# A fused convolution and mixer kernel: single batches transposed in twos of neighbouring blocks, one group's convolution buffers opened in two steps, first stages in smaller double-buffered pieces

## The chip, the core and the metric

The kernel runs on one core of one Trainium2 chip. Its time is the device time of one execution in microseconds (us); lower is better. The engines are named as in the profile: PE is TensorE's matmul stream and PEld its weight loads, ACT is ScalarE, DVE is VectorE, POOL is GpSimd, SP is SyncE, which here only issues DMAs.

## The reference, cut to what matters

```python
# x (8, 4096, 192), weight (8 heads, 7 taps); w = softmax of weight over the taps
x_pad = concat([zeros(B, 6, D), x], axis=1)
x[b, s, h, g] = sum over k of w[h, k] * x_pad[b, s + k, h, g]     # causal convolution, 24 columns a head
h  = relu(x.T @ w_tok1) @ w_tok2          # token mixing: 4096 -> 256 -> 4096, per batch
u  = x + h.T
h2 = relu(u @ w_ch1) @ w_ch2              # channel mixing: 192 -> 1536 -> 192, per token
out = u + h2
```

All values are float32. The kernel keeps the precision by splitting operands into a rounded part ("hi") and a rest ("lo") and adding three products, hi by hi, hi by lo and lo by hi.

## The kernel before

**Groups.** The eight batches are worked in five groups: batch 0, batch 1, and the pairs 2-3, 4-5 and 6-7. A single batch has `nb == 1`, a pair `nb == 2`. 4096 tokens are 32 blocks of 128; a tile is `TJ` = 4 blocks (512 tokens), and a batch has 8 tiles, q0 to q7.

**First stages** (`stage1`, for one group while the group before it runs its tiles). The convolution runs in four parts of 8 blocks for each batch (q2 = 0 to 3). `load` brings raw tokens, columns in two halves, `raw0` and `raw1`. `taps` gives head by head the first tap to ACT (line 608) and the other six to DVE (line 610), accumulating in `xc`. `store` writes `xc` to DRAM (`xcd`, line 634). Then token mixing's first matmul: for each quad of four blocks, `t1_load` fetches the weights (one `t1` buffer for a pair, two for a single batch), and for the pair 2-3, the first one, `t1_hi` (ACT, line 659) and `t1_lo` (DVE, line 663) split them and a store keeps the split (`t1p`) for later pairs. For pairs `split_hi` (ACT, 675) and `split_lo` (DVE, 679) split `xc` into one buffer `xhl`. `mix` multiplies into two accumulators `ps_a`: line 691 for a single batch, lines 695 to 697 for a pair, 24 matmuls a quad.

**Tiles.** Each tile runs in this order on PE: `channel1` (line 865, 72 matmuls at a time on half-height operands, results through ACT 904 into hi and DVE 905 into lo), `mix2` of the next tile (800 to 805; DVE adds its result to `u`, lines 810 and 812 for a single batch, 815 for a pair), the first half of `channel2` (917 and 918; DVE sums in 921 and 922), `transposed` of the next tile (828 on PE, 830 on ACT for hi, 831 on DVE for lo, into `own`), the second half of `channel2`, and the store. So the transposes of the next tile have the second half of `channel2` between them and the `channel1` that reads them.

A single batch's `u` has every block's 192 columns twice: DVE's second add (812) broadcasts them, so that one 128-row transpose delivers 64 columns in the lower and the same 64 columns in the upper partitions. `channel1` needs them in both places.

**Who sets the order.** `Background` keeps a model clock for PE and one for DVE. Each foreground step calls `fg` with its cost; `fill` then pops items of the next group's first stages from their streams, as long as the model's DVE is not ahead. Items have a `gate` (a time when their input may be there) and a `lag`. What is left when a group's last tile begins is forced by `finish()` ahead of the next group's first `channel1`. Each engine runs its instructions in the order written. The decode of the second token-mixing weights (lines 164 to 180, a staging copy on ACT in 1006, a store in 1008) is also such a stream, in batch 0's tiles.

Of the kernel before, what the change touches and what calls it, by code (L numbers as in the profile page):

```python
# [34 lines left out]
class Background:  # L35
# [28 lines left out]
    def fill(self, until):  # L64
        for s in self.streams:
            while s["items"] and s["items"][0].eager:
                self.pop(s)
        while self.dve < self.pe + until:
# [9 lines left out]
            if not ready:  # L78
                return
# [33 lines left out]
def conv_mixer_kernel(ctx: ExitStack, tc: tile.TileContext, x, weight, w_tok1, w_tok2, w_ch1, w_ch2, out):  # L113
    nc = tc.nc
# [12 lines left out]
    TJ = 4  # L127
    NT = NJ // TJ
# [6 lines left out]
    def f32(ap):  # L135
# [20 lines left out]
        dram.tile([P, len(g), NJ, D], F32, name=f"xcd{i}") for i, g in enumerate(GROUPS)  # L156
# [25 lines left out]
    class Decoder:  # L182
# [27 lines left out]
        def b(self, st, hi, lo, view=lambda v: v):  # L210
            return decode_b(view(st["top"]), hi, lo)

# [142 lines left out]
    def stage1_first(pe, p0, pd, late, load_u, load_next, after, hooks):  # L355
# [21 lines left out]
        xf = xcd[0][:, 0]  # L377
# [119 lines left out]
        def xc_store(c):  # L497
            nc.gpsimd.dma_start(out=xf[:, chunks[c].start:chunks[c].stop], in_=xcs[c])
# [76 lines left out]
    def stage1(gi, pool):  # L575
# [13 lines left out]
        def load(q2, part):  # L589

            ds = slice(part * DH, (part + 1) * DH)
            raw = pool.tile([P, RB + HALO, nb, DH], F32, name=f"raw{part}")
# [31 lines left out]
        def taps(q2, h, k):  # L624
            st = states[q2]
            if k == 0 and h == 0:
                st["xc"] = pool.tile([P, RB * nb, D], F32, name="xc", bufs=2)
# [3 lines left out]
        def store(q2):  # L631
            xc = states[q2]["xc"].rearrange("p (j b) d -> p j b d", b=nb)
            for i in range(nb):
                nc.gpsimd.dma_start(out=xcd[gi][:, i, q2 * RB:(q2 + 1) * RB], in_=xc[:, :, i])
            mark("conv", q2)

        def t1_load(n):
            q2, q = divmod(n, RB // TJ)
            js = slice(q * TJ, (q + 1) * TJ)
# [5 lines left out]
            if nb == 1:  # L645
                t1 = mp.tile([P, TJ, 1, JT], F32, name="t1", bufs=2)
                nc.sync.dma_start(out=t1, in_=part(top))
            elif gi == 2:
                t1 = mp.tile([P, TJ, 2, JT], F32R, name="t1")
                nc.sync.dma_start(out=f32(t1[:, :, 1:2]), in_=part(top))  # L650
            else:
                t1 = mp.tile([P, TJ, 2, JT], F32R, name="t1")
# [8 lines left out]
        def t1_lo(q2, q):  # L661
            t1 = states[q2]["t1", q]
            nc.vector.tensor_tensor(out=t1[:, :, 1], in0=f32(t1[:, :, 1]), in1=f32(t1[:, :, 0]), op=ALU.subtract)
            js = slice(q * TJ, (q + 1) * TJ)
# [4 lines left out]
        def split_hi(q2, q):  # L669
            st = states[q2]  # L670
            v = st["xc"][:, q * TJ * nb:(q + 1) * TJ * nb, :]
            xhl = mp.tile([P, 2, TJ * nb, D], F32R, name="xhl")
# [9 lines left out]
        def mix(q2, q, kc):  # L682
            t1 = states[q2]["t1", q]
            ms = slice(kc * P, (kc + 1) * P)
            for j in range(TJ):
                n = q2 * RB + q * TJ + j
                a, z = n == 0, n == NJ - 1
                ps = accs[kc][:, :nb * D]
                if nb == 1:
                    xc = states[q2]["xc"]  # L690
                    nc.tensor.matmul(out=ps, lhsT=t1[:, j, 0, ms], rhs=xc[:, q * TJ + j, :], start=a, stop=z)  # L691
# [9 lines left out]
        last_q = RB // TJ - 1  # L701
        for part in range(2):
            convolving.append(Item(lambda part=part: begin(0, part), eager=True))
        mixing.append(Item(lambda: t1_load(0), eager=True))
        for q2 in range(NS):
            for h in range(0, H, 2):
                for k in range(K):
                    it = Item(lambda a=(q2, h, k): taps(*a), cost=2 * (RB * nb * G / 0.96 + 130) if k else 0)
                    if h % HH == 0 and k == 0:
                        it.lag = 100  # L710

                        def gate(q2=q2, h=h):
                            if h == 0 and q2 > 1 and ("split" if nb > 1 else "mixed", q2 - 2, last_q) not in done:
                                return None
                            return done["load", q2, h // HH] + 2e3 + 2e3 * nb

                        it.gate = gate
                    convolving.append(it)
# [3 lines left out]
            for q in range(last_q + 1):  # L722
                a = (q2, q)
                n = q2 * (last_q + 1) + q
                if gi == 2:
                    mixing.append(Item(lambda a=a: t1_hi(*a), lag=300, gate=lambda n=n: done["t1", n] + (5e3 if n else 14e3)))
                    mixing.append(Item(lambda a=a: t1_lo(*a), cost=TJ * JT / 0.96, lag=1300))
                if nb > 1:
                    mixing.append(Item(lambda a=a: split_hi(*a), lag=300, gate=lambda q2=q2: done.get(("conv", q2))))
                    mixing.append(Item(lambda a=a: split_lo(*a), cost=TJ * nb * D / 0.96, lag=500 + 700 * nb))  # L730
# [46 lines left out]
    def tokens(u, i):  # L777
        return u[:, :, :, i]
# [338 lines left out]
```

## Time and profile before

| | us |
|---|---|
| median of 3 runs (lowest, highest) | 2102.41 (2100.42, 2102.64) |
| the profiled execution, its own time | 2103.08 |
| its span in the profile | 2101.3 |
| PE busy | 2059.8 (98%) |
| DVE busy | 1344.5 (64%) |
| ACT busy | 731.4 (35%) |

The span runs from the first to the last instruction of the profiled execution; the 1.8 us beside it in that execution's own time lie around the span. PE is busy nearly everywhere; DVE is close to full in the first quarter of the span, where batch 0's tiles share it with the convolution of batch 1 and the weight decode, and less so behind it.

### The profile page before, as it was taken

Reading aid. Unit: us, or ns where it says so; the run is one execution under the profiler, and the core shown is the slowest. Engines: PE = TensorE matmul, PEld = TensorE weight load, DVE = VectorE, ACT = ScalarE, POOL = GpSimd, SP = SyncE. Lnnn points to the kernel's source line nnn. Section 1 sums busy time; section 2 is a strip of 40 time slices with the busy share of each in tenths; the row PEclk is TensorE's granted clock in tenths of the full one; section 3 lists DMA queues with packets and bytes.
Section 4 is the critical chain, followed back from the end, with each engine's and each line's share of the span. In section 5 each row is a group of like instructions: output and inputs, shape, how many; then the busy total and the mean of one; then the engine's idle time right before and its main releaser. Section 6 shows DMA issues by size and latency. Waiting matters only on the chain.

```text
span 2101.3 us, 35971 instructions
## 1 busy us (share of the span) xinstructions
PE 2059.8 (98%) x15338; PEld 1901.4 (90%) x15338; DVE 1344.5 (64%) x2556; ACT 731.4 (35%) x1191; POOL 101.4 (5%) x170
## 2 busy tenths in 40 slices
PE   5999999999979999999999999999999999999999
PEld 5889999999979999999999999999999999999998
DVE  5799978888949888488444785444444444444443
ACT  3455543333324343333233333332232322233222
POOL 1100000000010000000000000000000000000000
PEclk9999999999989999999999999999999999999999
DMA  9735553545365563454222353222112122222210
GB/s 314 253 119 154 193 163 102 164 149 175 113 189 149 166 199 92 134 147 134 74 66 86 101 175 108 66 66 66 44 51 65 47 66 66 58 66 66 66 31 16
DMA packets 255808, 239.55 MB, mean 114 GB/s; under 512 B 203862, under 2 KB 214614, under 8 KB 251040
## 3 DMA queue, kind: packets, MB, share of 16 engines
q1 hardware_dynamic: 240240, 155.79, 25.5%
q0 software_dynamic: 15408, 81.45, 12.3%
q8 instruction: 121, 1.98, 0.4%
q14 instruction: 39, 0.32, 0.0%
HBM read 147.03 MB, written 71.30 MB: 104 GB/s over the span
## 4 chain that ended last, share of the span: by engine, by line
PE 95%; DVE 3%; DMA 1%; ACT 1%; issue 0%; POOL 0%; ACTq 0%; DVEq 0%
PE ps_x L865 38%; PE ps_x L917 28%; PE ps_x L918 12%; PE ps_x L828 2%; PE ps_x L803 2%; PE ps_a L696 2%; PE ps_a L697 2%; PE ps_a L695 2%; PE ps_x L805 2%; PE ps_x L804 2%; PE ps_x L800 1%; PE ps_a L415 1%; PE ps_a L691 1%; DVE xc L610 1%; PE ps_x L482 1%; PE ps_x L483 1%
## 5 line engine op out<-in xcount | busy, mean ns | idle before, releaser
L917 PE MATMUL ps_x<-w,hh 128*128 128x384 f32 x3024 | 873.9, 360 | 0.0
L918 PE MATMUL ps_x<-w,hl 128*128 128x192 f32 x3024 | 756.9, 250 | 0.0
L904 ACT ACTIVATE hh<-ps_x 128x512 fp32r<-128x512 f32 x756 | 410.2, 597 | 811.3 <-PE ps_x L865 811.3
L905 DVE SCALAR_TENSOR_TENSOR hl<-ps_x,hh 128x512 fp32r<-128x512 f32 x756 | 485.0, 685 | 246.2 <-ACT hh L904 245.9
L865 PE MATMUL ps_x<-own,w_hi 64*128 64x512 f32 x2880 | 609.0, 391 | 0.1
L918 PEld LDWEIGHTS ps_x<-w,hl 128*128 128x128 f32 x3024 | 577.4, 191 | 0.1
L917 PEld LDWEIGHTS ps_x<-w,hh 128*128 128x128 f32 x3024 | 567.7, 188 | 9.1 <-DVE hl L905 8.4
L865 PEld LDWEIGHTS ps_x<-own,w_hi 64*128 64x128 f32 x2880 | 427.5, 185 | 56.8 <-issue 5.8
L865 PE MATMUL ps_x<-other,w_hi 64*128 64x512 f32 x1728 | 452.0, 390 | 0.0
L610 DVE SCALAR_TENSOR_TENSOR xc<-raw,cw,xc 128x384 f32<-128x384 f32 (+1 forms) x768 | 386.3, 562 | 20.3 <-ACT xc L608 20.3
L865 PEld LDWEIGHTS ps_x<-other,w_hi 64*128 64x128 f32 x1728 | 314.5, 184 | 32.5 <-issue 3.8
L921 DVE TENSOR_TENSOR osb<-ps_x,u 128x192 f32<-128x192 f32 x252 | 89.8, 356 | 392.2 <-PE ps_x L918 392.0
L865 PE MATMUL ps_x<-own,w_lo 64*128 64x512 f32 x1440 | 326.7, 388 | 0.0
L865 PE MATMUL ps_x<-other,w_lo 64*128 64x512 f32 x864 | 242.3, 386 | 0.0
L865 PEld LDWEIGHTS ps_x<-own,w_lo 64*128 64x128 f32 x1440 | 216.7, 185 | 26.1
L830 ACT CAST own<-ps_x 128x512 fp32r<-128x512 f32 x120 | 63.0, 594 | 335.1 <-PE ps_x L828 335.1
L865 PEld LDWEIGHTS ps_x<-other,w_lo 64*128 64x128 f32 x864 | 158.9, 184 | 15.4
L922 DVE TENSOR_TENSOR osb<-ps_x,osb 128x192 f32<-128x192 f32 x252 | 90.2, 358 | 8.7
L831 DVE TENSOR_TENSOR own<-ps_x,own 128x512 fp32r<-128x512 f32 x120 | 75.7, 684 | 10.1 <-ACT own L830 9.9
L929 POOL DMA_DIRECT2D out_dram<-osb x63 | 36.8, 585 | 899.4 <-DVE osb L922 863.4
L695 PE MATMUL ps_a<-xhl,t 128*128 128x384 f32 x192 | 66.9, 348 | 8.7 <-ACT xhl L675 8.7
L696 PE MATMUL ps_a<-xhl,t 128*128 128x384 f32 x192 | 66.5, 346 | 2.5 <-DVE xhl L679 2.5
(106 smaller groups left out, 1513.4 us busy)
## 6 DMA issues: line engine op xcount, KB each, us to landing
raw<-in_x_dram SPq DMA_DIRECT2D x56, 672.0 KB, 8.0
t<-t2d SPq DMA_DIRECT2D x64, 512.0 KB, 4.7
u<-xcd SPq DMA_DIRECT2D x63, 384.0 KB, 5.7
out_dram<-osb POOLq DMA_DIRECT2D x63, 384.0 KB, 5.0
xcd<-xc POOLq DMA_DIRECT2D x31, 768.0 KB, 7.9
other<-own POOLq DMA_DIRECT2D x24, 768.0 KB, 5.4
t<-t1p SPq DMA_DIRECT2D x16, 1024.0 KB, 5.2
t<-t1d SPq DMA_DIRECT2D x16, 512.0 KB, 4.7
```

The source lines that it names most:

```text
L610: nc.vector.scalar_tensor_tensor(out=dst, in0=src, scalar=cw[:, h, k:k + 1], in1=dst, op0=ALU.mult, op1=ALU.add)
L695: nc.tensor.matmul(out=ps, lhsT=wh, rhs=xh, start=a, stop=False)
L696: nc.tensor.matmul(out=ps, lhsT=wh, rhs=xl, start=False, stop=False)
L830: nc.scalar.copy(out=own[:, 0, c], in_=ps)
L831: nc.vector.tensor_tensor(out=own[:, 1, c], in0=ps, in1=f32(own[:, 0, c]), op=ALU.subtract)
L865: nc.tensor.matmul(out=ps, lhsT=w1[w][rows, c, p * P:(p + 1) * P], rhs=t[h][rows, v, c], start=n == 0, stop=n == len(prods) - 1,)
L904: nc.scalar.activation(out=h["hh", f], in_=ps, func=AF.Relu)
L905: nc.vector.scalar_tensor_tensor(out=h["hl", f], in0=ps, scalar=0.0, in1=f32(h["hh", f]), op0=ALU.max, op1=ALU.subtract)
L917: nc.tensor.matmul(out=ps[:, :2 * D], lhsT=h["hh", f][:, ts], rhs=w2[:, f, :], start=n == 0, stop=False)
L918: nc.tensor.matmul(out=ps[:, :D], lhsT=h["hl", f][:, ts], rhs=w2[:, f, :D], start=False, stop=z)
L921: nc.vector.tensor_tensor(out=rows(osb[:, j]), in0=rows(ps[:, :D]), in1=tokens(u, i)[:, j], op=ALU.add)
L922: nc.vector.tensor_tensor(out=osb[:, j], in0=ps[:, D:2 * D], in1=osb[:, j], op=ALU.add)
```

## The change

1. `transposed` for a single batch takes two neighbouring blocks of 64 columns in one 128-row transpose: 6 transposes a tile in the place of 12. `u` now holds the blocks in twos (`new_u`), and the second add of `mix2` writes 192 columns instead of 384. Each half of the partitions is evicted apart: ACT's hi (line 864 of the changed kernel) and DVE's lo (865), and four ACT copies (868) carry each half's columns over to the other half.
2. `xcd` and the loads and stores on it are laid out for that (two DMAs for each store and each load of `u`).
3. The convolution buffers of the pair 2-3 stand in two pools. The first is opened by a `through` item when the decode's last store has been issued, the second at the end of batch 0.
4. The pieces of token mixing's first matmul are `MJ` = 2 blocks instead of 4; `t1` has two buffers (three for a single batch), `xhl` two, and the loads run two pieces ahead.
5. `fill` pops an item without cost even when the model's DVE is ahead, and lets eager items wait for their gate; the first taps of the next two heads stand ahead of the third tap of the heads before.

```diff
 def fill(self, until):
-            while s["items"] and s["items"][0].eager:
+            while s["items"] and s["items"][0].eager and self.may(s):
...
-        while self.dve < self.pe + until:
+        while True:
...
-            if not ready:
+            ready = [s for s in ready if not s["items"][0].cost] or ready
+            if not ready or (ready[0]["items"][0].cost and self.dve >= self.pe + until):
                 return
...
+    MJ = 2
...
-        dram.tile([P, len(g), NJ, D], F32, name=f"xcd{i}") for i, g in enumerate(GROUPS)
+        dram.tile([P, 2, NJ * len(g) // 2, D], F32, name=f"xcd{i}") for i, g in enumerate(GROUPS)
...
-                t1 = mp.tile([P, TJ, 1, JT], F32, name="t1", bufs=2)
+                t1 = mp.tile([P, MJ, 1, JT], F32, name="t1", bufs=3)
...
-                t1 = mp.tile([P, TJ, 2, JT], F32R, name="t1")
+                t1 = mp.tile([P, MJ, 2, JT], F32R, name="t1", bufs=2)
...
-            xhl = mp.tile([P, 2, TJ * nb, D], F32R, name="xhl")
+            xhl = mp.tile([P, 2, MJ * nb, D], F32R, name="xhl", bufs=2)
...
-                if n + 1 < NJ // TJ:
-                    mixing.append(Item(lambda n=n: t1_load(n + 1)))
+                if n + 2 < NJ // MJ:
+                    mixing.append(Item(lambda n=n: t1_load(n + 2)))
...
             if nb == 1:
-                one = uj[:, :, 1]
-                nc.vector.tensor_tensor(out=one, in0=rows(ps[:, :D]), in1=one, op=ALU.add)
-                lo, both = (v.unsqueeze(2).to_broadcast([P, ND, 2, D2]) for v in (rows(ps[:, D:2 * D]), one))
-                nc.vector.tensor_tensor(out=uj, in0=lo, in1=both, op=ALU.add)
+                uj = tokens(nb, u, 0, j)
+                nc.vector.tensor_tensor(out=uj, in0=rows(ps[:, :D]), in1=uj, op=ALU.add)
+                nc.vector.tensor_tensor(out=uj, in0=rows(ps[:, D:2 * D]), in1=uj, op=ALU.add)
...
+        halves = [low, high]
+        if nb == 1:
+            to = own.rearrange("p k c (j b t) -> p k (c j) b t", b=2, t=P)
+            NP2 = TJ // 2
+            for c0 in range(0, ND, 2):
+                n = min(2, ND - c0) * NP2
+                ps = ps_x.tile([P, TT], F32, name="ps_x")
+                for m in range(n):
+                    cols = u[:, m % NP2, c0 + m // NP2].rearrange("p b d -> p (b d)")
+                    nc.tensor.transpose(out=ps[:, m * P:(m + 1) * P], in_=cols, identity=ident)
...
+                for b, half in enumerate(halves):
+                    hi, lo = (to[half, k, at, b] for k in range(2))
+                    nc.scalar.copy(out=hi, in_=v[half])
+                    nc.vector.tensor_tensor(out=lo, in0=v[half], in1=f32(hi), op=ALU.subtract)
+            for k in range(2):
+                for b, half in enumerate(halves):
+                    nc.scalar.copy(out=to[halves[1 - b], k, :, b], in_=f32(to[half, k, :, b]))
+            return [(own, own)]
...
+        def through():
+            decode_ctx.close()
+            conv_pool(0)
+            starts[2] = stage1(2, lambda k: cps[k])
+        stores.append(Item(through))
+        bg.add(decode_items(Decoder(td, TT, 2, 2), jobs), lead=0.1, group=1)
```

On ACT, at the end of batch 1, between the last `channel2` and the first `channel1` of the pair 2-3 (`own` is the transposed tile, `t` the first token-mixing weights, `xhl` the split of `xc`, `h` the mixed result, `hh` `channel1`'s hi). Before:

```order
L608 ACTIVATE xc<-raw_5437,cw 128x16x24 x2
L830 CAST own<-ps_x 128x512 x3
L659 CAST t_6031<-t_6031 128x4x256
L675 CAST xhl<-xc 128x1536
L659 CAST t_6191<-t_6191 128x4x256
L675 CAST xhl<-xc 128x1536
L345 ACTIVATE h_379<-ps_a_3543 128x384
L345 ACTIVATE h_379<-ps_a_3544 128x384
L904 ACTIVATE hh_6233<-ps_x 128x512 x4
```

Of the change:

```order
L665 CAST t_5845<-t_5845 128x2x256
L681 CAST xhl<-xc_5320 128x768
L665 CAST t_6087<-t_6087 128x2x256
L864 CAST own<-ps_x 64x4x128 x2
L864 CAST own<-ps_x 64x2x128 x2
L868 CAST own<-own 64x6x128 x4
L681 CAST xhl<-xc_5320 128x768
L665 CAST t_6182<-t_6182 128x2x256
L681 CAST xhl<-xc_5320 128x768
L665 CAST t_6280<-t_6280 128x2x256
L681 CAST xhl<-xc_5320 128x768
L354 ACTIVATE h_379<-ps_a_3591 128x384
```

Two quads of 4 blocks have become three pieces of 2 behind the copies of `own`, with the first piece's weights already split; no tap stands among them any more. The next fence shows what the eight copies of `own` on ACT wait for in a tile of the change (PE is the transposes, DVE the lo of line 865):

```order
L864 CAST own<-ps_x 64x4x128 [waits PE_49]
L864 CAST own<-ps_x 64x4x128 [waits DVE_49]
L864 CAST own<-ps_x 64x2x128 [waits PE_49]
L864 CAST own<-ps_x 64x2x128 [waits DVE_49]
L868 CAST own<-own 64x6x128 [waits Activation_49] x2
L868 CAST own<-own 64x6x128
L868 CAST own<-own 64x6x128 [waits DVE_49]
```

The copy of the second half waits each time for DVE's lo of the first half.

On DVE, in batch 0's tile q6, from the additions of `mix2` for tile q7 on. Before:

```order
L810 TENSOR_TENSOR u<-ps_x,u 128x3x64
L812 TENSOR_TENSOR u<-ps_x,u 128x384
L921 TENSOR_TENSOR osb<-ps_x,u 128x192
L922 TENSOR_TENSOR osb<-ps_x,osb 128x192
L921 TENSOR_TENSOR osb<-ps_x,u 128x192
L922 TENSOR_TENSOR osb<-ps_x,osb 128x192
L831 TENSOR_TENSOR own<-ps_x,own 128x512 x3
```

Of the change:

```order
L834 TENSOR_TENSOR u<-ps_x,u 128x3x64
L835 TENSOR_TENSOR u<-ps_x,u 128x3x64
L618 SCALAR_TENSOR_TENSOR xc_3095<-raw_3032,cw,xc_3095 128x16x24 x8
L966 TENSOR_TENSOR osb<-ps_x,u 128x192
L967 TENSOR_TENSOR osb<-ps_x,osb 128x192
L618 SCALAR_TENSOR_TENSOR xc_3095<-raw_3032,cw,xc_3095 128x16x24 x6
L966 TENSOR_TENSOR osb<-ps_x,u 128x192
L967 TENSOR_TENSOR osb<-ps_x,osb 128x192
L618 SCALAR_TENSOR_TENSOR xc_3095<-raw_3032,cw,xc_3095 128x16x24 x2
L865 TENSOR_TENSOR own<-ps_x,own 64x4x128 x2
L865 TENSOR_TENSOR own<-ps_x,own 64x2x128 x2
```

Sixteen taps of the pair 2-3 now stand ahead of the lo of tile q7.

## Rows read from the trace of the kernel before

**Rows 1.** The page of the whole program: the span, the engines' busy times with shares and instruction counts, and the chain that ended last, by engine.

```profile
span 2101.3 us, 35971 instructions
PE 2059.8 (98%) x15338; PEld 1901.4 (90%) x15338; DVE 1344.5 (64%) x2556; ACT 731.4 (35%) x1191; POOL 101.4 (5%) x170
PE 95%; DVE 3%; DMA 1%; ACT 1%; issue 0%; POOL 0%; ACTq 0%; DVEq 0%
```

**Rows 2.** PE's timeline at the end of batch 1, from the last matmul of `channel2` to the first of the pair's `channel1`: start and duration in us, engine, line, tiles and shapes, count, and in brackets the idle time before with its releaser.

```profile
584.85 0.25 PE L918 MATMUL ps_x<-w,hl 128*128 128x192 f32 x1
...
601.41 0.69 PE L695 MATMUL ps_a<-xhl,t 128*128 128x384 f32 x1 [7.24 <-ACT xhl L675]
...
609.55 0.33 PE L696 MATMUL ps_a<-xhl,t 128*128 128x384 f32 x1
609.73 0.34 PE L697 MATMUL ps_a<-xhl,t 128*128 128x384 f32 x1
609.99 0.96 PE L865 MATMUL ps_x<-own,w_hi 64*128 64x512 f32 x6
```

**Rows 3.** The chain of waits in the same stretch, in order of time: start and duration in us, and the work.

```profile
594.20 4.63 DMA t<-t1d
598.94 1.04 ACT t L659
599.98 1.38 ACT xhl L675
601.39 1.77 DVE xhl L679
```

**Rows 4.** Windows: a stretch in us and its length, then busy time of PE, PEld, DVE, ACT and POOL (with counts), the granted TensorE clock, DMA share and GB/s. The first is a tile of batch 0, the second a tile of batch 1, the third five us at the end of batch 1.

```profile
240.10:275.90 35.80, 35.70 (x266) 32.79 (x265) 35.42 (x89) 13.18 (x27) 1.31 (x2) 1.00 0.40 123
...
508.30:542.80 34.50, 34.50 (x259) 31.58 (x258) 29.66 (x55) 12.20 (x21) 2.86 (x4) 1.00 0.59 186
...
600.00:605.00 5.00, 2.49 (x7) 2.09 (x8) 2.98 (x2) 1.35 (x1) 0.55 (x1) 0.50 1.24 306
```

**Rows 5.** Groups of instructions by line and form, whole program: line, engine, operation, tiles, shapes, count, then busy us, mean ns of one, and the idle time before.

```profile
L828 PE MATMUL ps_x<-ident,u 128*128 128x128 f32 x480 | 62.3, 279 | 4.5 <-DVE u L812 4.2 <-PE ps_x L801 0.2
L830 ACT CAST own<-ps_x 128x512 fp32r<-128x512 f32 x120 | 63.0, 594 | 335.1 <-PE ps_x L828 335.1
L831 DVE TENSOR_TENSOR own<-ps_x,own 128x512 fp32r<-128x512 f32 x120 | 75.7, 684 | 10.1 <-ACT own L830 9.9
L836 ACT CAST other<-own 64x1536 fp32r<-64x1536 f32 x48 | 68.5, 1472 | 0.9
L610 DVE SCALAR_TENSOR_TENSOR xc<-raw,cw,xc 128x384 f32<-128x384 f32 x576 | 318.0, 612 | 20.0 <-ACT xc L608 20.0
L608 ACT ACTIVATE xc<-raw,cw 128x384 f32<-128x384 f32 x96 | 53.4, 614 | 2.1 <-DVE xhl L679 2.0
L812 DVE TENSOR_TENSOR u<-ps_x,u 128x384 f32<-128x384 f32 x64 | 35.7, 558 | 2.2
L810 DVE TENSOR_TENSOR u<-ps_x,u 128x192 f32<-128x192 f32 x64 | 22.3, 348 | 1.1 <-PE ps_x L801 1.1
```

**Rows 6.** Timeline of a tile of batch 1: the transposes on PE, their copies on ACT and DVE, and the `channel1` that reads them.

```profile
508.27 1.47 PE L828 MATMUL ps_x<-ident,u 128*128 128x128 f32 x12
508.90 1.57 ACT L830 CAST own<-ps_x 128x512 fp32r<-128x512 f32 x3 [11.81 <-PE ps_x L828]
509.52 1.89 DVE L831 TENSOR_TENSOR own<-ps_x,own 128x512 fp32r<-128x512 f32 x3 [0.30 <-ACT own L830]
...
516.47 0.73 PE L865 MATMUL ps_x<-own,w_hi 64*128 64x512 f32 x4
```

**Rows 7.** The chain of waits there: start, duration, work.

```profile
508.43 1.31 PE ps_x L828 x12
```

**Rows 8.** Timeline of a tile of batch 0: the transposes, the taps on DVE ahead of their lo, the lo, and the `channel1` that reads them.

```profile
240.11 1.47 PE L828 MATMUL ps_x<-ident,u 128*128 128x128 f32 x12
...
242.09 2.06 DVE L610 SCALAR_TENSOR_TENSOR xc<-raw,cw,xc 128x192 f32<-128x192 f32 x6
...
244.73 1.88 DVE L831 TENSOR_TENSOR own<-ps_x,own 128x512 fp32r<-128x512 f32 x3
...
248.31 0.73 PE L865 MATMUL ps_x<-own,w_hi 64*128 64x512 f32 x4
```

**Rows 9.** The chain at the start of batch 0's first tile, and a window there (columns as in rows 4).

```profile
77.24 0.57 DVE u L812
...
77.86 2.18 PE ps_x L828 x9
80.04 12.01 PE ps_x L865 x87
...
80.00:85.00 5.00, 5.00 (x31) 3.97 (x32) 3.61 (x5) 1.70 (x4) 0.00 (x0) 0.68 1.21 254
```

**Rows 10.** Around batch 0's tile q6: SP's timeline with the raw loads of the pair 2-3, the DMA view of that stretch (KB each, median us to landing), and the chain.

```profile
300.18 6.97 SPq L598 DMA_DIRECT2D raw<-in_x_dram  x4
...
raw<-in_x_dram SPq DMA_DIRECT2D x4, 672.0 KB, 7.2
...
311.20 1.31 PE ps_x L828 x12
...
319.31 12.49 PE ps_x L865 x108
```

More of the change, by code (lines that the diff above doesn't have):

```diff
@@ L211, in b, with xc_out @@
             return decode_b(view(st["top"]), hi, lo)
+    def xc_out(gi, j0, n, xc):
+        nb = len(GROUPS[gi])
+        at = slice(j0 * nb // 2, (j0 + n) * nb // 2)
+        for i in range(2):
+            nc.gpsimd.dma_start(out=xcd[gi][:, i, at], in_=xc.rearrange("p (j b) d -> p j b d", b=2)[:, :, i])
     def w1_job(c):
@@ L699, in mix, with loaded, tap, gate @@
                 mark("mixed", q2, q)
[L701 to L704, printed above, removed]
+        last_q = RB // MJ - 1
+        def loaded(q2, part):
+            at = done.get(("load", q2, part))
+            return None if at is None or pools(q2 % 2) is None else at + 2e3 + 2e3 * nb
+        def tap(q2, h, k):
+            it = Item(lambda: taps(q2, h, k), cost=2 * (RB * nb * G / 0.96 + 130) if k else 0)
+            if h % HH == 0 and k == 0:
+                it.lag = 100
+                def gate():
+                    if h == 0 and q2 > 1 and ("split" if nb > 1 else "mixed", q2 - 2, last_q) not in done:
+                        return None
+                    return loaded(q2, h // HH)
+                it.gate = gate
+            convolving.append(it)
+        convolving.append(Item(lambda: begin(0, 0), eager=True))
+        second = [Item(lambda: begin(0, 1), eager=True, gate=lambda: None if pools(1) is None else 0.0)]
+        for n in range(2):
+            mixing.append(Item(lambda n=n: t1_load(n), eager=True))
         for q2 in range(NS):
+            tap(q2, 0, 0)
             for h in range(0, H, 2):
[L707 to L718, printed above, removed]
+                for k in range(1, K):
+                    if k == K // 2 and h + 2 < H:
+                        tap(q2, h + 2, 0)
+                    tap(q2, h, k)
                 if h % HH == HH - 2 and q2 + 1 < NS:
@@ L749, in stage1 @@
         bg.add(convolving, group=gi)
+        bg.add(second, group=gi)
         return start, finish
@@ L844, in first_load @@
     def first_load(xc):
[L845 to L846 removed]
+        u = new_u(1)
+        for i in range(2):
+            nc.gpsimd.tensor_copy(out=u[:, :, :, i], in_=xc[:, i:TJ:2].rearrange("p j (c d) -> p j c d", d=D2))
         first["u"] = None, u
```

100 lines of the change are left out of this document (50 added, 50 removed).

## The prediction

> **What bounds the kernel now.** I read the page first. PE is busy 2059.8 of 2101.3 us and makes 95% of the chain that ended last [rows 1]; so only two things move the time: PE work that goes away, and the few stretches in which PE waits. The windows by tile show how the load differs by place: a tile of batch 0 has DVE busy 35.42 of 35.80 us, a tile of batch 1 29.66 of 34.50, with PE full in both [rows 4]. The large hole is the end of batch 1. There `channel2` ends at 585.1 (584.85 + 0.25) and the pair's `channel1` begins at 609.99; in between stand only the 48 matmuls of two forced quads, the second of which waits 7.24 us [rows 2]. The chain names the cause in order: the weights' load, issued when the first quad's matmuls have given the one `t1` buffer free at 594.20, lands 4.63 us later, then 1.04 us of ACT split, 1.38 of `xhl` hi, 1.77 of lo [rows 3]. PE also drops to a granted clock of 0.50 there, the lower of its two levels [rows 4].
>
> The profiled execution took 2103.08 us, 0.67 above the median 2102.41; the span leaves 1.8 us outside, which the change does not touch. I sum signed differences against 2103.08 and take the same off the median.
>
> **Transposes saved.** 12 transposes take 1.31 us on the chain [rows 7], a pitch of 0.109 us each (their mean of 279 ns [rows 5] overlaps the next). Six fewer save 0.655 us a tile. Two single batches have 16 tiles; the first two lie in the start, treated apart below; tiles q2 to q7 of batch 0 and the eight of batch 1 are 14. The saving is PE's own only where PE is not made to wait by what the change adds.
>
> **The chain of halves.** Before, the lo of `own` was not needed until long after `channel1` had begun. Now ACT's copy of a second half waits for DVE's lo of the first, and `channel1`'s first matmul waits for the cross copies of all hi. Let T be the first transpose. By the tile of batch 1, ACT begins at T + 0.63, DVE's lo at T + 1.25, `channel1` at T + 8.20 [rows 6]. A half-height copy has as many elements per partition as a full one, so I give it the full one's mean: 0.59 on ACT and 0.68 on DVE for 4 blocks [rows 5], and for 2 blocks about 0.35 each, an estimate by the 192-wide add of 0.348 [rows 5]. A cross copy has half the elements of the 1472 ns copy of line 836 [rows 5], so 0.74. From the first lo: two lo and the ACT copy between them 0.68 + 0.59 + 0.68, then lo 3 and the ACT copy of the fourth half 0.35 + 0.35, then two cross copies 1.48; that makes 4.1, with gaps 4.25. All hi are ready at T + 5.5, all lo 1.5 later. `channel1` would start at T + 8.20 - 0.65 = T + 7.55. So in a tile like this there are 2.05 us to spare and nothing is lost: nine tiles bound by PE alone (q7 of batch 0, eight of batch 1) save 9 x 0.655 = **-5.9**. Bounds: 0 if each waits just what it saved. If DVE rows of the convolution stand ahead of a lo by more than 2.05 the tile waits: I put **+1** on batch 1 for that (0 to +5).
>
> **Batch 0's full tiles.** Where DVE is full, its lo starts late: at 244.73, behind six taps and two sums, 4.62 after T = 240.11, and `channel1` began at 248.31 [rows 8]. With the halves, hi is ready at 244.73 + 4.25 = 248.98 against a start of 247.65: 1.33 late. Five tiles (q2 to q6) are 6.6 lost against 5 x 0.655 = 3.3 saved, so +3.3. The second add of `mix2` falls from 558 to about 348 ns [rows 5], 0.84 a tile that DVE has earlier, against some 1.2 us of new gaps between ACT and DVE, in which neither works on this tile, less the part where DVE catches up over a tile. I take **+2**; from -3.3, all hidden, to +7.
>
> **The start.** In the first tile the transposes follow the adds at once: the last add ends at 77.81 and `channel1` starts at 80.04 [rows 9]. Here nothing covers the chain. With adds 0.84 shorter the last add ends at 77.0, three transposes behind it at 0.24 each (nine take 2.18 there) end at 77.7, and the halves of the last tile, two of whose copies are done, put `channel1` near 83.1: +3.1. The second tile saves about 1.6 (half of nine transposes and the shorter adds). The clock is granted at 0.68 from 80 to 85 [rows 9], so PE is slow there a little longer, +0.5. Together **+2** (-1 to +5).
>
> **Tile q7 of batch 0.** Its lo now stands behind 16 taps of the pair 2-3 whose raw tiles are loaded only after the decode's last store. Before, the raw loads were issued from 300.18 [rows 10], four of them with 7.2 us to landing; two of them first should land about 306. Then 4 first taps at 0.614 on ACT and 16 at 0.612 on DVE [rows 5], partly side by side, with the sums between, give the first lo at about 317.4 and hi at 317.4 + 4.25 = 321.7. `channel1` began at 319.31 [rows 10], less 0.66 is 318.65. That is +3.1; a PE that waits so long may fall to the lower clock as in rows 4, +1.5 for that. **+4.6** (0, if the raw tiles land early, to +10). What the earlier taps bring stands in the next term.
>
> **The end of batch 1.** The convolution of the pair is through a tile earlier and three pieces of 12 matmuls are forced instead of two quads of 24. A matmul at full clock takes 0.175 (609.55 to 609.73 [rows 2]). Before, 609.99 - 585.10 = 24.9 less 48 x 0.175 = 8.4 is 16.5 lost. After, with t = 0 at `channel2`'s end: piece 13 has its weights split, its matmuls run at once, 2.1. Only piece 15 must wait for a buffer, that of piece 13, so its load is issued at about 2.1 to 2.5 and lands 4.6 later [rows 3], at 7.1. Half of the split's 1.04 is 0.52, half of the 1.38 is 0.69, half of the 1.77 is 0.89 [rows 3]: lo is ready at 9.2, and 12 matmuls end at 11.3. Of that 36 x 0.175 = 6.3 is work: 5.0 lost. The difference is **-11.5**; bounds -16.5 (nothing waits) and -4.7 (a second piece waits as well: two loads, splits and a cold clock, 11.8 lost).
>
> The other edits cost nothing on the path: `u` loads in two DMAs are issued a tile ahead; the stores of `xc` in two parts are POOL's, which is busy 5% [rows 1]; smaller pieces add fixed costs to ACT (35%) and to DVE (64%) in tiles of pairs [rows 1], where PE is the bound. Without that cover, in batch 0, they are in the +7.
>
> **Sum.** -5.9 + 1 + 2 + 2 + 4.6 - 11.5 = -7.8. 2103.08 - 7.8 = 2095.3 for an execution like the profiled one; off the median, **2094.6**.
>
> **Rivals.** *A, all of it is hidden.* DVE catches up, the raw tiles land early, the start loses nothing: 14 x 0.655 = 9.2 and 11.5 saved, and 1 at the start: 2102.4 - 21.7 = 2080.7. For it: 2.05 us to spare in batch 1 [rows 6]. Against it: row 244.73 [rows 8]. *B, slower:* the chain of halves bounds every single tile. Its place is `channel1`'s first matmul; its price the time by which hi comes after T + 7.55, in 14 tiles. With a lo that starts at T + 5.7, 1.1 later than in rows 8, hi is 2.4 late: 14 x 2.4 = 33.6, less 9.2 saved, less 11.5, plus 2: +14.9, so 2117. It decides from (11.5 + 9.2 - 2) / 14 = 1.3 us a tile, just what rows 8 show for one; batch 1's DVE has 4.8 us free a tile [rows 4], against it. *C, the end of batch 1 keeps most of its hole:* the double buffer covers one load, the others still queue behind PE, and the term is -4.7: 2094.6 + 6.8 = 2101.4, no difference to be told. For it: on ACT the splits stand behind eight copies of `own` now. *T, a transpose saves more than its pitch.* If each cost PE its mean of 279 ns [rows 5], the 54 fewer in nine tiles would save 54 x 0.17 = 9.2 more: 2085.4. The twelve in 1.31 us [rows 7] speak against it. The Trainium skill, "TensorE: Matmul & The Clock Gate", "Part 4: PE-mode transpose", gives a 128x128 transpose as about 275 ns in a kernel and 390 ns alone. By that rule T would hold, by an estimate from its 275 ns; the trace agrees with it only in the mean of one record, not in the pitch.
>
> **How the numbers follow.** Forecast 0.54, A 0.15, B 0.12, C 0.17, T 0.02. A measurement of this kernel tells a difference from about 0.2%, 4.2 us, so faster is below 2098.2 and slower above 2106.6. The forecast's own range is 2088 to 2100, by the bounds of its terms taken as independent; the part above 2098.2 is about 0.07. Faster: 0.47 + 0.15 + 0.02 = 0.64; same: 0.07 + 0.17 = 0.24; slower: 0.12. The range leaves out B and about half of A: 2083 to 2103.
>
> **What would show it.** After the change: six transposes in some 0.66 us on the chain and 384 in all; `channel1` of batch 1 without idle time before it; in q2 to q6 a wait of about 1.3 us released by ACT's cross copies; in q7 one of 3; at the end of batch 1 a hole of about 5 us of idle with one load in the chain. The forecast is wrong if the cross copies release a wait in batch 1's tiles, if two loads are in the chain at its end, or if the raw tiles land well behind 306.

## The result: 0.9% slower

The changed kernel takes 2119.90 us (2119.76 to 2120.22), the kernel before beside it 2101.45: a ratio of 1.0088, interval 1.007 to 1.0105, some 18 us slower where 7.8 faster was forecast. The page after, span, busy times and the chain by engine, to set beside [rows 1]:

```profile
span 2118.0 us, 36089 instructions
PE 2059.5 (97%) x15242; PEld 1897.4 (90%) x15242; DVE 1341.1 (63%) x2604; ACT 794.3 (38%) x1303; POOL 115.8 (5%) x187
PE 78%; DVE 12%; ACT 4%; issue 2%; DMA 0%; POOL 0%; DVEq 0%; ACTq 0%; POOLq 0%; SPq 0%
```

PE is busy for as long as before in a longer span, although it runs 96 matmuls fewer, the transposes saved (15242 against 15338). DVE, 3% of the chain before, is now 12% of it, and ACT 4%. Everything happens before 630 us: the last tile of batch 1 starts its `channel1` 16.5 us later than before, and the span ends 16.7 later. One name has to be put right first. The `channel1` behind the hole at batch 1's end, at 609.99 in [rows 2], is that of batch 1's own last tile, not the pair's, as the text ahead of the result says: `finish()` runs ahead of the last tile. The length of the hole is the same by either name.

The starts of `channel1` on PE, tile by tile, against those of the profile before, give where it went (us; minus is a gain). A column ends where the `channel1` of its last tile starts; what a tile loses inside its own `channel1` counts for the next. "The hole" is the stretch at batch 1's end between the last `channel2` and the `channel1` behind it. "q0-q6 of batch 1" holds 2.1 us of mixing, twelve matmuls that stood in the hole before, in the runs whose hole has 36 of them (the change, e1, e3 to e5, e7, e9); in e8 the hole has 72, 24 more than before (4.2 us), in the other runs 48 as before.

| profile of | start, to q1 | q2-q6 of batch 0 | q7 | q0-q6 of batch 1 | last tile with the hole | whole span |
|---|---|---|---|---|---|---|
| the change | +2.0 | +14.0 | +3.6 | +6.6 | -9.7 | +16.7 |
| e1_first_stages | -2.1 | +7.6 | -1.3 | +5.7 | -10.2 | -0.1 |
| e2_paired | +2.4 | +13.9 | -0.1 | +0.3 | +4.5 | +21.0 |
| e3_hi_first | -0.9 | +9.0 | -0.5 | +1.2 | -11.4 | -2.1 |
| e4_pool_lo | +1.5 | +10.5 | +3.2 | +2.7 | -11.2 | +7.6 |
| e5_hi_first_pool | -0.7 | +6.8 | +0.8 | +4.2 | -11.2 | +1.0 |
| e6_paired_pool | +0.6 | +3.7 | +0.9 | -4.0 | +3.8 | +5.5 |
| e7_old_fill | 0.0 | +3.7 | +0.6 | +5.7 | -8.3 | +6.2 |
| e8_late_pools | -0.7 | +7.0 | +0.8 | -6.8 | +20.8 | +23.5 |
| e9_lead | -1.4 | +10.1 | +0.2 | +3.5 | -11.2 | +1.4 |
| e10_best | -2.1 | +8.5 | +0.4 | -2.7 | -9.5 | -5.2 |
| e11_best15 | -1.3 | +6.7 | +0.2 | -3.0 | -10.0 | -7.2 |
| e12_act15 | -1.7 | +8.4 | -0.5 | 0.0 | -9.6 | -3.3 |

The tiles of both single batches cost 24 us, 22 without the moved matmuls, instead of next to nothing; the hole gives back less than that. What PE waits for in those tiles, 105 to 590 us of the changed kernel (waiting line and releaser, us in total, times, longest):

```profile
PE ps_x L910 <- DVE osb L967: 5.9, 4, 2.6
PE ps_x L910 <- DVE hl L950: 4.2, 6, 1.5
PE ps_x L910 <- ACT own L868: 3.4, 3, 2.0
PE ps_x L826 <- DVE t2s L182: 2.7, 1, 2.7
```

Only the third row is the wait that the prediction priced, `channel1` for the cross copies. The others are PE waiting inside a tile for DVE to do its ordinary work: the sums that free a PSUM buffer, the lo of `channel1`, the weight decode. So the question is why DVE, as busy as before, is late. What DVE waits for, first the changed kernel in that stretch, then the kernel before from 105 to 580:

```profile
DVE hl L950 <- ACT hh L949: 17.0, 16, 1.9
DVE own L865 <- ACT own L864: 16.7, 30, 1.2
DVE xc L618 <- ACT xc L616: 11.7, 4, 4.5
DVE t L669 <- ACT t L665: 10.6, 4, 3.5
...
```

```profile
DVE hl L905 <- ACT hh L904: 19.0, 21, 2.2
DVE osb L921 <- PE ps_x L918: 18.3, 13, 5.3
DVE own L831 <- ACT own L830: 3.8, 10, 1.2
DVE xc L610 <- ACT xc L608: 3.5, 4, 1.1
```

Before, DVE idled on PE's `channel2` (18.3 us of slack). Now it idles on ACT, 16.7 us for the hi of `own`, 11.7 for a first tap, 10.6 for the split of the first weights, and does its work late. One tile of batch 1 shows how; parts of ACT's timeline, then DVE's, then PE's (start, duration, line, idle time before):

```profile
494.81 0.58 ACT L864 CAST own<-ps_x 64x512 fp32r<-64x512 f32 x1 [8.74 <-PE ps_x L858]
496.49 0.98 ACT L864 CAST own<-ps_x 64x512 fp32r<-64x512 f32 x2 [1.10 <-DVE own L865]
499.46 0.37 ACT L864 CAST own<-ps_x 64x256 fp32r<-64x256 f32 x1 [2.00 <-DVE own L865]
499.74 3.40 ACT L868 CAST own<-own 64x768 fp32r<-64x768 f32 x4
503.16 0.62 ACT L665 CAST t<-t 128x512 fp32r<-128x512 f32 x1
```

```profile
495.79 0.67 DVE L865 TENSOR_TENSOR own<-ps_x,own 64x512 fp32r<-64x512 f32 x1
497.11 0.69 DVE L865 TENSOR_TENSOR own<-ps_x,own 64x512 fp32r<-64x512 f32 x1 [0.65 <-ACT own L864]
497.84 1.15 DVE L618 SCALAR_TENSOR_TENSOR xc<-raw,cw,xc 128x384 f32<-128x384 f32 x2
499.87 0.43 DVE L865 TENSOR_TENSOR own<-ps_x,own 64x256 fp32r<-64x256 f32 x1 [0.44 <-ACT own L864]
503.81 0.69 DVE L669 TENSOR_TENSOR t<-t 128x512 fp32r<-128x512 f32 x1 [3.52 <-ACT t L665]
```

```profile
510.13 0.93 PE L910 MATMUL ps_x<-own,w_hi 64*128 64x512 f32 x5 [1.75 <-DVE osb L967]
```

The two engines hand halves to each other until 499.8. Then ACT runs the four cross copies, 3.40 us, and only then the split of `t`, for which DVE stands still 3.52 us. Behind that instruction in DVE's queue are taps and the tile's sums; a sum frees the PSUM buffer that `channel1` wants, and PE loses 1.75 us at 510. The cross copies were not late for `channel1` here at all: it begins at 503.76, when they are done.

PE loses more than it waits. After its longest waits the granted clock falls. The windows below (columns as in [rows 4]) are of the changed kernel; the first holds a wait of 2.66 us for the decode at 170 and the time behind it, the second stands behind a wait of 2.60 us for a sum at 232, the third behind one of 2.04 us for the cross copies at 339:

```profile
169.00:174.00 5.00, 3.63 (x18) 3.63 (x19) 4.86 (x15) 2.85 (x6) 1.51 (x2) 0.78 0.13 12
234.00:239.00 5.00, 5.00 (x36) 4.70 (x34) 5.00 (x11) 2.53 (x6) 0.00 (x0) 0.73 0.69 233
339.00:344.00 5.00, 5.00 (x31) 5.00 (x32) 1.31 (x4) 3.14 (x6) 0.75 (x1) 0.66 0.88 231
```

Before, the clock is granted at 1.00 from the `channel1` of q1 to that of q6 (117.66 to 284.15) and in q7; a value between 0.50 and 1.00 is a stretch with both levels in it. Around 173 us `channel2` starts a pair of matmuls every 0.54 us, at 175.5 every 0.29. The three windows alone are worth some 4 us of PE's time (an estimate: what the clock is short of 1.00, times 5 us each). The waits in the four rows come to 16 us, so the 22 us are those waits, the clock, and a rest that is not traced, less the transposes saved.

### The profile page after: what moved, and what is told of

Its sections match the earlier page's. It is cut to its first block, busy times and chain, and to the rows that moved or that the text cites. A ratio compares the mean times of both kernels' runs of the same rounds, so it can differ in the third digit from the quotient of the medians.

```text
span 2118.0 us, 36089 instructions
## 1 busy us (share of the span) xinstructions
PE 2059.5 (97%) x15242; PEld 1897.4 (90%) x15242; DVE 1341.1 (63%) x2604; ACT 794.3 (38%) x1303; POOL 115.8 (5%) x187
## 4 chain that ended last, share of the span: by engine, by line
PE 78%; DVE 12%; ACT 4%; issue 2%; DMA 0%; POOL 0%; DVEq 0%; ACTq 0%; POOLq 0%; SPq 0%
PE ps_x L910 33%; PE ps_x L962 24%; PE ps_x L963 11%; DVE xc L618 5%; DVE hl L950 2%; PE ps_x L828 2%; PE ps_x L830 2%; PE ps_x L829 2%; PE ps_x L874 1%; PE ps_a L702 1%; PE ps_a L701 1%; PE ps_a L703 1%; ACT own L868 1%; DVE own L865 1%; ACT own L864 1%
## 5 line engine op out<-in xcount | busy, mean ns | idle before, releaser
L910 PE MATMUL ps_x<-own,w_hi 64*128 64x512 f32 x2880 | 625.4, 394 | 19.2 <-ACT own L868 8.1
L910 PEld LDWEIGHTS ps_x<-own,w_hi 64*128 64x128 f32 x2880 | 437.8, 186 | 81.7 <-issue 12.4
L618 DVE SCALAR_TENSOR_TENSOR xc<-raw,cw,xc 128x384 f32<-128x384 f32 (+1 forms) x768 | 387.9, 561 | 14.2 <-ACT xc L616 13.9
L910 PE MATMUL ps_x<-own,w_lo 64*128 64x512 f32 x1440 | 334.6, 390 | 0.0
L910 PEld LDWEIGHTS ps_x<-own,w_lo 64*128 64x128 f32 x1440 | 224.5, 186 | 24.5
L876 ACT CAST own<-ps_x 128x512 fp32r<-128x512 f32 x72 | 37.7, 594 | 246.7 <-PE ps_x L874 246.7
L616 ACT ACTIVATE xc<-raw,cw 128x384 f32<-128x384 f32 (+1 forms) x128 | 66.1, 573 | 33.1 <-DVE xhl L685 15.3
L864 ACT CAST own<-ps_x 64x512 fp32r<-64x512 f32 (+1 forms) x64 | 30.4, 475 | 109.7 <-PE ps_x L858 71.6
L701 PE MATMUL ps_a<-xhl,t 128*128 128x384 f32 x192 | 66.2, 345 | 5.4 <-ACT xhl L681 5.4
```

The lines of the kernel that those rows point to most:

```text
L616: nc.scalar.activation(out=dst, in_=src, func=AF.Copy, scale=cw[:, h, 0:1])
L618: nc.vector.scalar_tensor_tensor(out=dst, in0=src, scalar=cw[:, h, k:k + 1], in1=dst, op0=ALU.mult, op1=ALU.add)
L701: nc.tensor.matmul(out=ps, lhsT=wh, rhs=xh, start=a, stop=False)
L864: nc.scalar.copy(out=hi, in_=v[half])
L910: nc.tensor.matmul(out=ps, lhsT=w1[w][rows, c, p * P:(p + 1) * P], rhs=t[h][rows, v, c], start=n == 0, stop=n == len(prods) - 1,)
```

## The experiments

**Parts apart.** The changed kernel without parts 1 and 2 (e1), and these parts alone (e2). For e2 this is left out of the changed kernel, with all that goes with it:

```diff
-    MJ = 2
...
-        stores.append(Item(through))
...
-            ready = [s for s in ready if not s["items"][0].cost] or ready
```

For e1 the transposes of before are put back, with `u` and `xcd` as before:

```diff
-                    cols = u[:, m % NP2, c0 + m // NP2].rearrange("p b d -> p (b d)")
...
+                cols = u[:, j, c].rearrange("p b d -> p (b d)")
```

> The change without its transposes: parts 3 to 5 alone (early convolution buffers, pieces of two blocks, first taps ahead), with the twelve transposes a tile and the broadcast add of before. Theory one (the eight copies of own on ACT hold up ACT's queue, and DVE, which waits in order behind first taps, decode copies and splits on ACT, loses that time): batch 0's tiles q2 to q6 take about as long as before (+0 to +3 us in all, where the changed kernel has +14), batch 1's tiles +2 (twelve matmuls moved into them), the hole at batch 1's end stays 9 to 10 us shorter; sum about 2094 us (2089 to 2099). Rival (the new order of the first stages costs the tiles, the transposes are innocent): the tiles lose as in the changed kernel, and the sum is about 2112.

> Parts 1 and 2 alone: transposes in twos with their layout, first stages as before. Theory one (ACT's block of copies): start +2, batch 0's tiles +10 to +14, batch 1's +2 to +5, the hole at its end as before; sum about 2119 us (2113 to 2125). Rival (the order of the first stages): the transposes save 0.655 us in 14 tiles, the start costs 2; sum about 2094.

Measured: e1 2104.23 us (1.0009 of before, 1.0000 to 1.0018); e2 2123.64 (1.0104, 1.0089 to 1.0119). The transposes alone are the loss, and more than the whole of it; e2 lies in the range expected by theory one, though batch 1's tiles lose 0.3 instead of 2 to 5 and the hole did not stay as before. e1 was expected near 2094 and missed: the hole is 10.2 us shorter, but batch 0's tiles lose 7.6. PE's waits on ACT's `xhl` and on the loads of the weights there, 105 to 640 us:

```profile
PE ps_a L697 <- ACT xhl L677: 5.2, 1, 5.2
PE ps_a L693 <- DMA t<-t1d: 3.4, 2, 2.6
```

The first is the hole's. The second is the mixing of batch 1, whose weights now come in loads of half the size and stand behind raw tiles and decode loads (the load waited for at 216 us is issued at 208.05, behind a raw tile at 205.82 and a decode load at 207.61). So the first stages' parts are worth nothing by themselves. In e2 the hole grows by 4.5: in the chain there the cross copies on ACT (to 601.9 us) stand ahead of the weights' split, and DVE's last taps, which the split of `xhl` waits for, behind that. They are not the whole cause, since e6, below, keeps 3.8 with the copies on POOL.

**The alternation.** Only the order in which the copies are written:

```diff
-                for b, half in enumerate(halves):
-                    hi, lo = (to[half, k, at, b] for k in range(2))
-                    nc.scalar.copy(out=hi, in_=v[half])
+                for b, half in enumerate(halves):
+                    nc.scalar.copy(out=to[half, 0, at, b], in_=v[half])
+                for b, half in enumerate(halves):
+                    hi, lo = (to[half, k, at, b] for k in range(2))
                     nc.vector.tensor_tensor(out=lo, in0=v[half], in1=f32(hi), op=ALU.subtract)
```

> The changed kernel with ACT's two hi copies of a PSUM tile written ahead of DVE's two lo, so that no ACT copy waits for DVE's lo in between. Theory one, the part of it that is the alternation: DVE idles 1.08 us less in each single tile and the cross copies start 0.6 to 1.3 us earlier; about 0.5 to 1.0 us in each of 14 tiles, so 2106 to 2113 us. If the cross copies alone (3.4 us of ACT) are the cost: 2118 to 2120.

Measured: 2101.31 us (0.9998 of before, 0.9989 to 1.0008), 18.6 less than the change. The direction was expected, the size not: the estimate took DVE's idle time alone, 1.08 us a tile. PE's busy time, with the same 15242 matmuls, falls from 2059.5 to 2050.6 us, so 8.9 of the 18.8 us by which the profiled span is shorter are matmuls that take less time. The mean granted clock, 0.993 in the profile of the change and 0.995 here, is part of that; the rest of it stays open. The same tile in this run, ACT and DVE:

```profile
481.90 1.96 ACT L863 CAST own<-ps_x 64x512 fp32r<-64x512 f32 x4 [8.57 <-PE ps_x L858]
483.76 1.69 ACT L869 CAST own<-own 64x768 fp32r<-64x768 f32 x2
486.16 1.69 ACT L869 CAST own<-own 64x768 fp32r<-64x768 f32 x2 [0.71 <-DVE own L866]
487.87 0.62 ACT L665 CAST t<-t 128x512 fp32r<-128x512 f32 x1
...
488.52 0.69 DVE L669 TENSOR_TENSOR t<-t 128x512 fp32r<-128x512 f32 x1 [1.94 <-ACT t L665]
```

ACT's four copies of hi are done 1.96 us after the first began instead of 5.0, and the split of `t` starts 5.97 us after it instead of 8.35. DVE's idle time there falls from 3.52 to 1.94, on top of what it no longer loses between the halves. All the work queued behind moves up by both. Batch 0's tiles still lose 9.0, most of which e1 loses without the transposes too.

**The cross copies' engine.** On POOL the two lo copies (e4), or all four with hi first (e5).

```diff
-                    nc.scalar.copy(out=to[halves[1 - b], k, :, b], in_=f32(to[half, k, :, b]))
+                    nc.gpsimd.tensor_copy(out=to[halves[1 - b], k, :, b], in_=f32(to[half, k, :, b]))
```

> The changed kernel with the two cross copies of lo on POOL instead of ACT: 1.7 us of ACT's block gone in each tile. Theory one: what DVE waits for behind them (first taps, splits) comes 1.7 us earlier; in 14 tiles 0.5 to 1.2 us each, so 2103 to 2113 us, if a POOL copy takes under about 3 us and so ends before channel1's third set of products. If POOL is slower than that, channel1 waits for lo and the time is 2120 or more. Rival (the order of the first stages): no change, 2119 to 2120.

> The changed kernel with hi copies ahead of lo, and all four cross copies on POOL (0.83 to 0.94 us each there in the run with the lo ones on POOL, as on ACT). Theory one (what is left of the loss with hi first is DVE waiting behind the cross copies on ACT, 1.94 us in a tile of batch 1 for the first weights' split, 1.78 in one of batch 0 for a first tap): another 2 to 6 us gone, 2096 to 2100. Rival (what is left is the order of the first stages alone): as with hi first, 2101 to 2102.

Measured: e4 2111.49 (1.0044, 1.0027 to 1.0061), 8.4 less than the change, as expected of ACT's block. e5 2103.09 (1.0008, 0.9998 to 1.0017), not the 2 to 6 less than e3 that was expected. The gain is there in q2 to q6 (+6.8 instead of +9.0) and given back in two ways. In q7 DVE's lo stand behind the pair's taps, and so late that inside `channel1` PE waits 2.7 us for POOL's lo copies. And DVE's taps become slower, in the groups by line of e3 and then of e5 (busy us, mean ns):

```profile
L618 DVE SCALAR_TENSOR_TENSOR xc<-raw,cw,xc 128x384 f32<-128x384 f32 x576 | 319.3, 611 | 7.4 <-ACT xc L616 7.2
L618 DVE SCALAR_TENSOR_TENSOR xc<-raw,cw,xc 128x192 f32<-128x192 f32 x192 | 69.0, 412 | 4.2 <-ACT xc L616 4.0
L866 DVE TENSOR_TENSOR own<-ps_x,own 64x512 fp32r<-64x512 f32 x32 | 22.0, 687 | 9.5 <-ACT own L863 9.2
```

```profile
L618 DVE SCALAR_TENSOR_TENSOR xc<-raw,cw,xc 128x384 f32<-128x384 f32 x576 | 326.6, 625 | 9.5 <-ACT xc L616 9.3
L618 DVE SCALAR_TENSOR_TENSOR xc<-raw,cw,xc 128x192 f32<-128x192 f32 x192 | 74.9, 444 | 0.2
L869 POOL CAST own<-own 64x768 fp32r<-64x768 f32 x64 | 56.2, 879 | 193.0 <-ACT own L863 179.0 <-DVE own L866 11.3
L866 DVE TENSOR_TENSOR own<-ps_x,own 64x512 fp32r<-64x512 f32 x32 | 22.0, 687 | 10.4 <-ACT own L863 10.2
```

56.2 us of POOL copies cost DVE's taps 13.2 us, while the lo of `own`, which reads PSUM, costs the same 687 ns. By the Trainium skill, "GPSIMD Engine Reference", "1. Specifications", POOL shares its SBUF interfaces with VectorE and contends with instructions that have two SBUF inputs; the taps have two (`raw` and `xc`), the lo one, and the trace agrees.

**The transposes alone, mended.** Hi first and POOL, without parts 3 to 5 (the two edits above on e2).

> Transposes in twos alone, first stages as before, with hi copies ahead of lo and the cross copies on POOL. If the chain between ACT and DVE is what the transposes cost: the start +1, tiles -5 to -9, the hole at batch 1's end as before, so 2094 to 2099 instead of the 2123.6 with the copies as in the change. If something else in them costs (the layout's loads, the half-height work on DVE): 2105 or more.

Measured: 2106.91 (1.0030, 1.0020 to 1.0040); 16.7 less than e2, but not the 2094 to 2099; it is on the side of the rival, by which something else in the transposes costs (2105 or more). Batch 1 gains 4.0, close to the 7 x 0.655 = 4.6 of the transposes saved. Batch 0's tiles lose 3.7, of which 3.1 is one wait of `mix2` for the decode (DVE's subtraction, line 180 here), and the hole is 3.8 longer: its first wait for `xhl` takes 4.5 us instead of 1.4, because the last taps, which the split waits for, are late on DVE, in part beside POOL's copies. DVE's and POOL's timelines there:

```profile
576.26 2.20 DVE L616 SCALAR_TENSOR_TENSOR xc<-raw,cw,xc 128x384 f32<-128x384 f32 x4
...
583.10 3.27 DVE L616 SCALAR_TENSOR_TENSOR xc<-raw,cw,xc 128x384 f32<-128x384 f32 x4
...
581.20 3.69 POOL L853 CAST own<-own 64x768 fp32r<-64x768 f32 x4 [24.60 <-ACT own L847]
```

Four taps, two of them beside POOL's copies, take 3.27 us where four without them take 2.20: the two take 1.11 and 1.18 us, the others 0.61. That is 1.1 of the 3.1 us; the rest is other work ahead on DVE.

**The popping rule and the early pools.**

```diff
-            ready = [s for s in ready if not s["items"][0].cost] or ready
```

for e7, with the `while` of before, and for e8, which opens both pools at the end of batch 0,

```diff
-        stores.append(Item(through))
...
+                        conv_pool(0)
                         conv_pool(1)
```

> As the run with hi first and POOL, with the rule of before for popping items (nothing is popped while the model's DVE is ahead). If the new rule costs batch 0's tiles (work on ACT and loads popped early, the weight decode late): 3 to 7 us less than that run in tiles q2 to q6. If the rule is innocent: the same within 2 us, or more where the pieces at batch 1's end are later.

> As the run with hi first and POOL, with both convolution pools of the pair 2-3 opened at the end of batch 0, as before, and no taps of the pair in batch 0's tile q6. If the early opening is what shortens the hole at batch 1's end: 5 to 10 us more than that run, all of it there. If double buffers and small pieces do that alone: the same within 2 us at the end of batch 1, and 1 to 3 less in tiles q6 and q7 of batch 0.

Measured: e7 2110.30 (1.0044, 1.0027 to 1.0061), slower than e5; its q2 to q6 lose 3.7 instead of 6.8, as expected of a costly rule, but the hole is 2.9 longer and the pairs behind lose 4.4. So the rule costs batch 0 and pays elsewhere. e8 2126.55 (1.0118, 1.0103 to 1.0133): the last tile with its hole goes from -11.2 to +20.8, far over the 5 to 10 expected, and batch 1's other tiles gain 10.9, 6.3 of it 36 matmuls that are now in the hole. PE's longest wait:

```profile
PE ps_a L702 <- DVE xhl L685: 16.0, 4, 14.6
```

Without the early taps the convolution itself reaches the end of batch 1. So the double buffers and small pieces do not shorten the hole without the early opening; whether the early opening would do it without them was not run.

**A mended version.** e9 gives the decode's stream a lead of 0.2 instead of 0.1 on e5 (`fill` pops from the stream whose share done, less its lead, is smallest, so a larger lead brings the decode forward); e10 adds one hi cross copy on ACT beside one on POOL, and lets the pair's first taps in 10 us later, both in one run; e11 is e10 with a lead of 0.15; e12 is e11 with all cross copies on ACT. The edits of e11 (the other lines of the copies as in e3):

```diff
-            return None if at is None or pools(q2 % 2) is None else at + 2e3 + 2e3 * nb
+            return None if at is None or pools(q2 % 2) is None else at + (16e3 if gi == 2 and q2 == 0 else 2e3 + 2e3 * nb)
...
+                    engine = nc.gpsimd.tensor_copy if k or b else nc.scalar.copy
+                    engine(out=to[halves[1 - b], k, :, b], in_=f32(to[half, k, :, b]))
...
-        bg.add(decode_items(Decoder(td, TT, 2, 2), jobs), lead=0.1, group=1)
+        bg.add(decode_items(Decoder(td, TT, 2, 2), jobs), lead=0.15, group=1)
```

> As the run with hi first and POOL (2103.1), with the weight decode's stream given a lead of 0.2 instead of 0.1, so that DVE's last subtraction of a decoded part stands some ten instructions ahead of where it stands now before the next tile's second mix. If the order of the first stages is what still costs batch 0 (the second mix of tile q3 waits 2.8 us for that subtraction; the last decode store, and with it the raw loads of the pair 2-3, is late): 2.5 to 6 us less, 2097 to 2100.5. If batch 0's tiles are simply full on DVE, the time moves elsewhere: 2102 to 2104.

> As the run before in this call, with the hi cross copies one on ACT and one on POOL side by side, and the first taps of the pair 2-3 let in 10 us later, when their raw tiles have landed. If DVE waiting in tile q6 for raw tiles is what costs tile q7 (3.0 us of waiting for the cross copies on POOL): another 2 to 4 us less, and 0.8 at the start: 2093 to 2098. If not: as the run before.

> As the second run of this call with a lead of 0.15: the order of batch 0 between the two others; the same theory gives 2093 to 2099, a rival by which any order of a full DVE costs the same gives 2101 to 2104.

> As the run with a lead of 0.15 (2096.2), with all four cross copies back on ACT. If POOL's copies cost little beyond their own time: DVE waits behind the cross copies again in the tiles of batches 0 and 1, 2 to 6 us more, 2098 to 2102. If what POOL's copies take from DVE's taps (444 instead of 412 ns for the 192-element ones, 625 instead of 612 for the others with four copies on POOL) weighs more than ACT's 1.7 to 2.5 us: 2 to 4 us less, 2092 to 2094.

Measured: e9 2104.25 (1.0011, 1.0002 to 1.0020): the wait for the decode is gone, and its time turns up as other waits for DVE in q1 to q5; the rival was right, and the lead alone is worth nothing. e10 2097.74 (0.9982, 0.9973 to 0.9991), in its range, though the two edits in it were not run apart and twelve matmuls are back in the hole. e11 **2096.20 (0.9976, 0.9966 to 0.9986)**, in its range too and 0.24% faster than the kernel before. No run has these edits without the transposes in twos, so how much of it the transposes are worth is not shown. e12 2099.07 (0.9988, 0.9979 to 0.9997), 2.9 more than e11, as expected if POOL's copies cost little, with the two intervals overlapping. By the profiles the difference is in batch 1's tiles (0.0 instead of -3.0) and in q2 to q6 (1.7 worse), so POOL seems worth its price once the taps of q7 are out of the way. With the copies back on ACT the taps take 613 and 413 ns again.

## Why the prediction was wrong, step by step

**What bounds the kernel, and the transposes' price: right.** Six fewer save their pitch: in e10 and e11 four of batch 1's tiles are 0.5 to 0.9 us shorter than before, around the 0.655 forecast. Rival T, 279 ns each, is out.

**The chain of halves: wrong in what was asked of it.** The prediction asked when hi is ready for `channel1`, found 2.05 us to spare, and called the rest free. That time was priced well: in the tile whose transposes begin at 362 us, both cross copies of hi are done 4.5 us after the first lo began, for 4.25 forecast, and in no tile of batch 1 does `channel1` wait for them. What was missed is the other side of each wait: DVE's instruction that waits for ACT holds up DVE's queue, and the block of cross copies holds up ACT's, with the weights' split, first taps and decode behind it, for which DVE waits in order. Batch 1 was put at +1 beside its share of the saving; without the 2.1 us of moved matmuls it is +4.5 instead of -3.6.

**Batch 0's full tiles: right place, +14.0 instead of +2**, and past the bound of +7. The term priced the late hi alone (1.3 us a tile, 6.6 in all) and took 1.2 us of new gaps as partly caught up. The wait that it priced comes to 1.3 us in the five tiles together. In tiles where DVE has nothing free, what it idles comes out at PE: from the `channel1` of q1 to that of q6 DVE is busy 160.8 of 180.6 us, before 161.1 of 166.5. PE's lower clock behind the waits is in that time too, and the term had nothing for it. That the mechanism is the waiting and not the work is shown by e3: same instructions, other order, 18.6 us less.

**The other edits: put at nothing on the path, and in batch 0 within the +7.** Parts 3 to 5 alone (e1) cost q2 to q6 7.6 us. The costs do not add up, since the transposes alone (e2) cost them 13.9 and both together 14.0.

**The start: right**, +2.0 forecast and +2.0 measured; its first tile +3.0 (+3.1).

**Tile q7 of batch 0: right in kind.** Its `channel1` starts 3.6 later, where 3.1 less the 0.66 saved was forecast, and by the forecast way: the raw tiles land at 321.2 and 323.3, which is 305 to 307 in the time of before (`channel1` of tile q6 starts 16.1 late), and `channel1` waits for ACT's cross copies:

```profile
338.87 1.64 PE L910 MATMUL ps_x<-own,w_hi 64*128 64x512 f32 x6 [2.04 <-ACT own L868]
```

The clock that the term put 1.5 on falls behind this wait, to the 0.66 shown above, 1.7 us by the same estimate. The sum is somewhat over the +4.6 and inside its bounds.

**The end of batch 1: right in kind, 8.6 lost instead of 5.0.** The chain there:

```profile
611.33 0.84 ACT xhl L681
612.20 0.97 DVE xhl L685
...
615.46 5.25 DMA t<-t1d
...
620.81 0.62 ACT t L665
621.42 0.74 ACT xhl L681
622.19 0.97 DVE xhl L685
```

One load in the chain, as forecast. But the first piece's matmuls do not run at once: its split stands behind the cross copies on ACT until 611.33, and its buffer is free 3.9 us after `channel2`'s end (611.54) instead of 2.1 to 2.5. The load takes 5.25 instead of 4.6, and part of the last matmuls runs at the lower clock (0.59 from 622 to 624, 0.64 from there to `channel1`). The term gave 7.9 of the 11.5.

**The rivals.** B, the slower one, gave 2117 against 2119.9, but by a wait at `channel1`'s first matmul; of the 16 us that PE waits in the four rows above, 3.4 are of that kind. It had the culprit, the chain between ACT and DVE, and the wrong victim, so that its number came near is luck; its condition, a lo that starts 5.7 us after the first transpose in every tile, is not what happened: the first lo starts 1.3 to 5.3 us after it. It was put at 0.12 by the 4.8 us that DVE has free in a tile of batch 1, and that slack does not help an engine that is made to stand still at the wrong time. C happened in part: the splits did stand behind the copies of `own`, and the hole gave back 7.9, between C's 4.7 and the forecast's 11.5. None of the three signs by which the forecast was to be known as wrong appeared: no cross copy releases a wait in batch 1's tiles, one load is in the chain, the raw tiles land at 305 to 307 in the time of before. They watched the wait that was priced and no other.

What stays open is why q2 to q6 still lose 7 us in the best version. It goes with parts 3 to 5: e1, which has only these, loses 7.6 there, e6, without them, 3.7, of which 3.1 is one wait for the decode, and e7, without the popping rule, 3.7. The waits are DVE's, and each change of order moved them; no run took parts 4 and 5 apart for the single batch.

## What to carry to other kernels

A wait that is added between two engines is priced by what is queued behind it on both, not by when the final consumer needs the data: list the instructions behind the waiting one, who waits for them, and whether that engine has slack just there. Where two engines take turns on pieces of a tile, write all of the first engine's pieces ahead of the second's; here that order alone was 18.6 us. Pieces of one change should be run apart: the part that lost hid the 10 us that another won at the end of batch 1, and that gain was eaten up in the tiles until the decode, the taps and the copies had been put in another order. And a wait of PE costs more than its length where the granted clock falls behind it.

## What had not been expected of the hardware

A 64x768 copy from one half of the partitions to the other takes POOL 0.88 us in the mean and ACT 0.83, so POOL is hardly slower for it. Its price is the 13 us that DVE's two-input taps lose beside 56 us of such copies; in e6 two taps beside them took 1.1 and 1.2 us instead of 0.61.
